# Grouping the value products of an attention and mixture-of-experts kernel by three key chunks instead of two

## The chip, the cores and the metric

One core of one Trainium2 chip runs the whole program. The metric is the device time of one execution in microseconds (us). The engines are named as in the profile: PE is the matmul engine (PEld its weight loads), DVE the vector engine, ACT the scalar engine, POOL the GpSimd engine, and SP issues DMAs.

## What is computed

Two batches, eight heads, 768 positions, head size 64, all in float32. Scores are masked by a six-bit hash of queries and keys:

```python
q_bits = (einsum('bhsd,dk->bhsk', q, proj) > 0)      # the same for k
mask = q_bucket[:, :, :, None] == k_bucket[:, :, None, :]
scores = where(mask, scale * q @ k.T, -1e9)
attn = exp(scores - max(scores)); attn = attn / (sum(attn) + 1e-9)
x = (attn @ v)                                        # to [1536, 512]
h = ((x @ w1) * (x @ w2)) @ w3;  y = h @ w_out        # dense layer
e = argmax(y @ w_gate + modality_bias[modality_id])   # one of 8 experts
out = gate * (relu(y @ W1[e]) @ W2[e])
```

The change lies in the attention part alone, which shares its time with the preparation of the dense layer (the product of w3 and w_out, called W34 here).

## The kernel before, in words

**Units and slots.** The function `body` handles pairs of heads: eight pairs, p = 0 to 7. A pair has twelve units of stage 1 and twelve units of stage 2. The main loop (`for i in range(NU + LEAD + NLAG + 1)`, NU = 96) runs over slots i. In slot i it issues, on each engine's queue in the order of the code, pieces of many things that are in different stages of progress. What follows is one slot, in that order.

- **Stage 1** of unit i (`stage_1`, L346 and L354, while i < 96): two matmuls give the scores of 128 queries against all keys, and DVE takes the row maximum (L354). After the last of every six units POOL makes the correction for the maxima of a half of the queries (L358 to L361, tile `fin`).
- **A step of the weight preparation on DVE** (`fill`): each of 40 raw weight pieces takes three DVE steps (L516, L517, L506), then for 24 of them an ACT copy and a POOL subtraction (L493, L494, `split`), which make the operands of W34. In a "long" slot, `fill` runs a second time here, and more `fill` calls stand behind stage 2 for slots outside the grouped region or when the list of steps is longer than two.
- **W34 matmuls** (`w34_step`, L599): up to nine 128x512 matmuls, by an allowance that grows by 3.35 each slot, and none in a long slot. After 24 matmuls a block is done. Then ACT copies it out (L602, `ev`), the next slot transposes it (`w34_t`, L574, `wt`), a later long slot does the gate matmuls (`w34_gate`, L582, `pg`), and the slot after that transposes those (`w34_sum`, L590, `pt`).
- **The transposes of the maxima** (`stage_f`, L366): three PE transposes bring the maxima of a half into the rows of the query operand, and two ACT copies (L369) write them there. They are issued in the slot `fi = i - 1` with `fi % 6 == 0`, so two slots after the last maximum of the half.
- **Value products** (`stage_a`, L392): the product of one key chunk's exponentials with the values, for both heads of the pair side by side in 64 columns each; four PE records of 385 columns. In slots with j = i - 9 from 18 to 97 they are issued only where `j % RUN == 1`, so two units together in every second slot.
- **Sums** (`stage_n`, L407): eight matmuls for the sums of a pair, in the slot NLAG units after its last unit of stage 2, then an ACT copy, DMAs and, for each batch, reciprocals on DVE (L419 to L424, the function `recip` from the list `late`).
- **Hashes** (`hash_half`, L259 and L272): for two coming pairs together, eight matmuls and one DVE operation per half of the positions, in the slots with i % 12 of 4 and 6 (`HASH`) of every second pair. The bits go to the operands by DMA (`d_bits`, from SP) in slots with i % 12 of 6 and 8.
- **Stage 2** of unit j (`stage_2`, L378, L379, L384): four matmuls give the transposed scores of one key chunk, ACT takes the exponential (L379) into one of four buffers `pt`, and POOL adds it to a running sum (L384).

**What couples the engines.** The two score tiles in PSUM (tag `s`) alternate between stage 1 and stage 2. So stage 1 of slot i + 1 waits for the maximum of slot i, and stage 2 of a slot waits for the exponential of the slot before. The tiles of `stage_f`, `w34_t`, `w34_gate`, `w34_sum`, `stage_n` and `hash_half` all have one PSUM buffer with the tag `m`, so each of them waits until ACT or DVE has read the one before.

**Long slots.** `grouped(i)` holds for slots 27 to 88, and `is_long(i)` for those of them that issue value products together. Before the change these are the even slots 28 to 88. `free_tail` puts the gate matmuls into a long slot that has no sums and (before) is not 1 modulo 6. The lower half of the queries (`q_lo`, L299 on DVE) is put at the head of the DVE list in slots with i % 12 = 6 and runs with the first `fill` of the next slot. In slots 78 to 89 `norm_0` (L656, L659, L661 on DVE) normalises the first quarter of the attention result. From slot 98 on, `moe_half` issues matmuls of the dense layer between the slots' other work.

The names that the change touches are these; everything else keeps its order.

Of the kernel before, what the change touches and what calls it, by code (L numbers as in the profile page):

```python
# [43 lines left out]
LEAD = 9  # L44
SOON = 17
AGE = 2
NLAG = 4
RUN = 2
NP = 4
BUSY = {4: (2, "m"), 5: (2, "m"), 6: (2, "a"), 7: (2, "a"), 8: (1, "a"), 9: (1, "a")}  # L50
GROUP = (18, 80)
AEND = 98
HASH = (4, 6)
PREL = 2
PREA = 2
SPLITS = (83, 84, 97, 98)
# [113 lines left out]
def body(tc, qT, kT, vP, w1d, w2d, w3d, wod, mod, wgate, mbias, e1, e2, cst, out):  # L170
# [65 lines left out]
    def load_pair(p):  # L236
        b, hp = divmod(p, HP)
        for nm, src in (("q", qT), ("k", kT)):
            t = r_raw([P, S])
            SP.dma_start(t, src[b, hp])  # L240
            raw_t[p, nm] = t
# [8 lines left out]
    def hash_half(pairs, half):  # L250
        hash_z(pairs, half)
        hash_bits(pairs, half)
# [88 lines left out]
    def stage_1(u):  # L341
        p, qt, hd = u
        q, k = head_t[p, hd, "q"], head_t[p, hd, "k"]
        s = ps("s", [P, 2, 512], f"m{p}_{qt}_{hd}")
        for half in range(2):
            PE.matmul(  # L346
                s[:, half, 0:HS], q[0:KROWS[hd], 0, qt * P:qt * P + P], k[0:KROWS[hd], 0, half * HS:half * HS + HS],
                start=True, stop=True,
            )
        if qt % 3 == 0 and hd == 0:  # L350
            nm_t[p, qt // 3] = r_nm([P, 32])
        nm = nm_t[p, qt // 3]
        at = 3 * (1 - hd) + qt % 3
        DVE.tensor_reduce(nm[:, at:at + 1], s[:, :, 0:HS], AX.XY, ALU.max, negate=True)  # L354
        if qt % 3 == 2 and hd == 1:
            v, fin = nm[:, 6:12], fins[qt // 3].bitcast(F32R).rearrange("p t (d c) -> p d t c", d=2)
            v3 = v.rearrange("p (d t) -> p d t", d=2)
            POOL.tensor_scalar(v, nm[:, 0:6], C_MASK / 2, None, ALU.is_lt)  # L358
            POOL.tensor_mul(v, v, nm[:, 0:6])
            POOL.tensor_copy(fin[:, :, :, 0], v3)  # L360
            POOL.tensor_sub(fin[:, :, :, 1], v3, fin[:, :, :, 0].bitcast(F32))  # L361
# [159 lines left out]
    def fill():  # L521
        if dq and isinstance(dq[0], int):
            dq[0:1] = piece(dq[0])
        if dq:
            dq.pop(0)()
# [13 lines left out]
    def grouped(i):  # L539
        return GROUP[0] <= i - LEAD < GROUP[1]  # L540

    def is_long(i):
        return grouped(i) and (i - LEAD) % RUN == 1

    def hashes(i):
        p, ph = divmod(i, 12)
        return p % 2 == 1 and p + 1 < NPAIR and ph in HASH

    def sums(i):
        n = i - LEAD - NLAG  # L550
        return 0 <= n < NU and n % 12 == 11

    def free_tail(i):
        while grouped(i) and (not is_long(i) or i % 6 == 1 or sums(i)):
            i += 1
        return i

# [13 lines left out]
    def w34_t(f, ev):  # L571
        t = ps("m", [P, 4, P], f"wt{f}")
        for c in range(4):
            PE.transpose(t[:, c, :], ev[:, c * P:c * P + P], ident)  # L574
        wT = r_wT([P, 4, P])
        ACT.copy(wT, t)
        tail_at.setdefault(free_tail(slot[0] + 1), []).append(lambda: w34_gate(f, wT))
# [35 lines left out]
    def w34_step(n, share=1):  # L613
        if 2 * slot[0] + share < w34_at[0]:
            return
        while n and done["w"] < len(w34q) and order.index(9 + 2 * w34q[done["w"]][0]) < done["n"]:
            w34q[done["w"]][1]()
            done["w"] += 1
            owed[0] -= 1
            n -= 1  # L620
            if done["w"] % 24 == 0:
                w34_at[0] = 2 * slot[0] + share + 2
                break
# [163 lines left out]
    sunits = [(p, half, c) for p in range(NPAIR) for half in range(2) for c in range(QT)]  # L787
    for i in range(NU + LEAD + NLAG + 1):
        slot[0] = i
# [54 lines left out]
        long = is_long(i)  # L844
        if i < NU:
            if p and ph == 9 and p + 3 < NPAIR:
                load_pair(p + 3)
            stage_1(units[i])
            fill()
            if long:  # L850
                fill()
        if p == 0 and ph in (1, 2):
            hash_z([1], ph - 1, "uw"[ph - 1])
# [7 lines left out]
        elif not long:  # L861
            quota = done["w"] + min(W34_MOST, int(owed[0]))
            w34_step(quota - done["w"], 0)
        fi = i if i <= 6 else i - 1
        if fi % 6 == 0 and 0 < fi <= NU and (i <= 6 or fi > 6):
            stage_f(*divmod(fi // 6 - 1, 2))
        for fn in todo_at.pop(i, []):
# [1 line left out]
        if hashes(i):  # L869
            for fn in tail_at.pop(i, []):  # L870
                fn()
        alone = not GROUP[0] <= j < AEND or j % RUN == 1
        while alone and next_a[0] <= min(j - AGE, NU - 1):
            stage_a(next_a[0])
            next_a[0] += 1
        for fn in tail_at.pop(i, []):
            fn()
        n = j - NLAG
        if i == NU + LEAD + 2:
# [3 lines left out]
        if hashes(i):  # L883
            hash_half([p + 1, p + 2], HASH.index(ph))
        if 0 <= j < NU and i != SOON:
# [664 lines left out]
```

## Time and profile before

| | |
|---|---|
| median of three executions | 673.7 us (673.34 to 673.91) |
| the profiled execution | 673.39 us, of which its span is 671.3 us |
| PE busy | 644.8 us, 96% of the span |
| DVE busy | 383.0 us, 57% |
| ACT busy | 319.4 us, 48% |
| POOL busy | 320.8 us, 48% |
| PE clock granted | full in all 40 slices of the page |
| slots 13 to 26 | 31.4 to 67.4 us after the span's start |
| slots 27 to 77 | 67.4 to 221.2 us |
| slots 78 to 90 | 221.2 to 261.0 us |

The span runs from the first instruction to the last; some 2 us of the device time lie around it. The slots are found in the trace by the first matmul of stage 1 (L346). Matmuls are pipelined, and each lasts longer in the trace than the distance to the next one, so that work on PE is read from start to start. A busy share says how long an engine had something to do, and not whether anybody waited for it.

### The profile page before, as it was taken

What the parts mean: (1) busy time and instruction counts of PE and PEld (TensorE: products, weight loads), DVE (VectorE), ACT (ScalarE), POOL (GpSimd) and SP (SyncE); (2) the same over time, 40 slices, a digit from 0 to 9 for tenths busy, and PEclk for the clock granted to TensorE, in tenths of its full rate; (3) what the DMA queues carried; (4) which work ended last, traced back from release to release, by engine and by line L of the source; (5) the groups of instructions that cost most, each with busy time, mean ns of one, the idle gap of its engine ahead of it and who ended that gap; (6) DMA issues with size and microseconds to landing.
All of it is one profiled execution on the core that took longest, in us unless ns stands there. A gap on an engine that the chain in (4) does not pass through costs nothing. (4 is left out here: it accounts for less than half of the span.)

```text
span 671.3 us, 10130 instructions
## 1 busy us (share of the span) xinstructions
PE 644.8 (96%) x3650; PEld 507.9 (76%) x3650; DVE 383.0 (57%) x573; ACT 319.4 (48%) x510; POOL 320.8 (48%) x291
## 2 busy tenths in 40 slices
PE   7998999999999999999999999999999999999995
PEld 2544666666666665687988988998888899899984
DVE  6798777667786999833521311211385865575550
ACT  7367575666556655753421211211124655565551
POOL 7598988686869777766241340420125012201110
PEclk9999999999999999999999999999999999999999
DMA  7747472664647484313301001000047886766630
GB/s 229 234 148 176 152 247 92 179 187 135 209 127 212 130 239 138 113 48 104 98 17 56 24 0 48 1 1 31 5 166 237 295 276 236 232 213 209 216 115 19
DMA packets 40663, 93.88 MB, mean 140 GB/s; under 512 B 6544, under 2 KB 11008, under 8 KB 40608
## 3 DMA queue, kind: packets, MB, share of 16 engines
q1 hardware_dynamic: 38528, 86.62, 41.7%
q0 software_dynamic: 2080, 6.56, 2.8%
q8 instruction: 31, 0.51, 0.3%
q14 instruction: 24, 0.20, 0.1%
HBM read 72.98 MB, written 12.94 MB: 128 GB/s over the span
## 5 line engine op out<-in xcount | busy, mean ns | idle before, releaser
L684 PE MATMUL ab<-x,w 128*128 128x384 f32 x512 | 135.3, 339 | 0.6 <-ACT ss L411 0.6
L384 POOL TENSOR_TENSOR acc<-acc,pt 128x770 f32<-128x770 f32 x64 | 119.9, 1874 | 21.5 <-ACT pt L379 19.9
L354 DVE TENSOR_REDUCE nm<-m 128x1 f32<-128x768 f32 x96 | 91.4, 955 | 49.7 <-PE m L346 49.2
L379 ACT ACTIVATE pt<-s 128x768 f32<-128x768 f32 x96 | 78.0, 812 | 71.9 <-PE s L378 69.7
L684 PEld LDWEIGHTS ab<-x,w 128*128 128x128 f32 x512 | 93.4, 188 | 5.8 <-issue 4.4
L378 PE MATMUL s<-q,k 128*128 128x384 f32 (+1 forms) x384 | 91.0, 359 | 4.0 <-ACT pt L379 3.8
L378 PEld LDWEIGHTS s<-q,k 128*128 128x128 f32 (+1 forms) x384 | 63.6, 189 | 38.7 <-issue 16.2
L696 POOL TENSOR_TENSOR g<-gf,g 128x384 fp32r<-128x384 f32 x32 | 32.9, 1029 | 125.1 <-ACT g L695 121.5
L684 PE MATMUL ab<-xlo,w 128*128 128x384 f32 x256 | 86.4, 338 | 0.0
L1214 DVE TENSOR_TENSOR eu<-er,eu 128x1024 fp32r<-128x1024 f32 x56 | 67.4, 1223 | 22.3 <-ACT eu L1213 20.8
L392 PE MATMUL a<-pt,v 128*64 128x385 f32 x384 | 74.5, 502 | 0.0
L1405 POOL DMA_INDIRECT out<-o,sidx x13 | 13.6, 1046 | 123.2 <-ACT o L1404 106.8
L1379 PE MATMUL e1F<-ex,eu 128*128 128x256 f32 x576 | 69.8, 282 | 0.5 <-DVE ex L1343 0.3
L1379 PEld LDWEIGHTS e1F<-ex,eu 128*128 128x128 f32 x576 | 69.2, 189 | 1.4 <-DVE ex L1343 0.5
L1397 PE MATMUL e2F<-eu,h 128*128 128x512 f32 x288 | 68.8, 394 | 0.0
L694 DVE TENSOR_TENSOR gf<-asb,ab 128x384 f32<-128x384 f32 x32 | 17.7, 554 | 84.0 <-PE ab L684 83.3
L1397 PEld LDWEIGHTS e2F<-eu,h 128*128 128x128 f32 x288 | 53.2, 188 | 11.2
L1213 ACT CAST eu<-er 128x1024 fp32r<-128x1024 f32 x56 | 57.6, 1047 | 5.9 <-DMA er<-e 5.4
L1023 PE MATMUL x2p<-w,g 128*128 128x512 f32 x240 | 57.4, 396 | 0.0
L346 PE MATMUL m<-k,q 78*128 78x384 f32 x192 | 52.4, 355 | 4.4 <-DVE nm L354 2.8
L1023 PEld LDWEIGHTS x2p<-w,g 128*128 128x128 f32 x240 | 44.8, 188 | 10.8 <-issue 0.6
L599 PE MATMUL w<-wo,w 128*128 128x512 f32 x192 | 49.0, 393 | 0.4 <-POOL w L494 0.4
(207 smaller groups left out, 869.5 us busy)
## 6 DMA issues: line engine op xcount, KB each, us to landing
er<-e SPq DMA_DIRECT2D x56, 512.0 KB
cr<-w3d SPq DMA_DIRECT2D x16, 512.0 KB
cr<-wod SPq DMA_DIRECT2D x8, 512.0 KB
cr<-w1d SPq DMA_DIRECT2D x8, 512.0 KB
wfd<-cT SPq DMA_DIRECT2D x16, 256.0 KB
cr<-w2d SPq DMA_DIRECT2D x8, 512.0 KB
st<-wfd SPq DMA_DIRECT2D x16, 256.0 KB
raw<-kT SPq DMA_DIRECT2D x8, 384.0 KB
```

The costliest lines, as they stand in the source:

```text
L346: PE.matmul(s[:, half, 0:HS], q[0:KROWS[hd], 0, qt * P:qt * P + P], k[0:KROWS[hd], 0, half * HS:half * HS + HS], start=True, stop=True,)
L354: DVE.tensor_reduce(nm[:, at:at + 1], s[:, :, 0:HS], AX.XY, ALU.max, negate=True)
L378: PE.matmul(s[:, hd, 0:HS], k[0:n, i, c * P:c * P + P], q[0:n, i, cl], start=(i == 0), stop=(i == 1))
L379: ACT.activation(pts[j % NP][:, :, 0:HS], s[:, :, 0:HS], AF.Exp, scale=SCALE)
L384: POOL.tensor_add(acc, pts[(j - 1) % NP] if c == 1 else acc, pts[j % NP])
L392: PE.matmul(a_t[p, half][64 * hd:64 * hd + 64, :], v[:, c, 64 * hd:64 * hd + 64], pts[j % NP][:, hd, :], start=(c == 0), stop=(c == QT - 1 ...
L684: PE.matmul(t, w12[j][:, st, c, fs], x[mv][:, c, :], start=(c == 0 and i == 0), stop=(c == 3 and i == 2))
L1023: PE.matmul(st["ps"], g_t[ch, f // 4][:, a, f % 4, i * P:i * P + P], w34[b][:, f, :], start=(f == 0 and k == 0), stop=(f == 7 and k == 2),)
L1213: ACT.copy(t[:, 0, sl], raw)
L1214: DVE.tensor_sub(t[:, 1, sl], raw, t[:, 0, sl].bitcast(F32))
L1379: PE.matmul(o[f], w[:, st, c, fs], x[:, mv, c, :], start=(c == 0 and i == 0), stop=(c == 3 and i == 2))
L1397: PE.matmul(o, h[:, st, f, sl], w[:, mv, f, :], start=(f == 0 and k == 0), stop=(f == 7 and k == 2))
```

## The change

Seven places, all in `body` and its constants:

```diff
-NLAG = 4
-RUN = 2
+NLAG = 5
+RUN = 3
...
-HASH = (4, 6)
+HASH = (4, 7)
...
     def free_tail(i):
-        while grouped(i) and (not is_long(i) or i % 6 == 1 or sums(i)):
+        while grouped(i) and (not is_long(i) or sums(i)):
             i += 1
         return i
...
             stage_1(units[i])
             fill()
-            if long:
+            for _ in range(RUN - 1 if long else 0):
                 fill()
...
-        fi = i if i <= 6 else i - 1
+        fi = i if i <= 6 else i - 2
         if fi % 6 == 0 and 0 < fi <= NU and (i <= 6 or fi > 6):
             stage_f(*divmod(fi // 6 - 1, 2))
```

Value products are issued for three units in every third slot (28, 31, ... 106). These slots are the long ones up to 88, so that W34 matmuls have two slots of three. A long slot has three DVE steps behind its maximum. The transposes of the maxima move one slot later, to the slots 14, 20, 26 and so on, which are never long. The sums of a pair and what hangs on them (the reciprocals in slot 65, now 66) move one slot later, the second half of the hashes from i % 12 of 6 to 7. Gate matmuls may stand in any long slot without sums. The loop has one more slot at its end.

## Rows read from the trace of the kernel before

**Rows 1.** Busy time by stretch: stretch and length, PE, PEld, DVE, ACT, POOL, then clock:

```profile
31.40:67.40 36.00, 32.10 (x165) 16.78 (x166) 31.61 (x41) 24.24 (x37) 31.92 (x28) 1.00 0.62 167
67.40:221.20 153.80, 149.09 (x840) 101.97 (x839) 110.72 (x144) 93.71 (x142) 122.41 (x100) 1.00 0.57 171
221.20:261.00 39.80, 36.45 (x203) 23.21 (x201) 38.29 (x47) 21.17 (x33) 28.46 (x27) 1.00 0.60 179
```

**Rows 2.** Timeline of PE, slots 26, 27, 28: start, length, line, operation, count, idle before:

```profile
65.40 0.51 PE L346 MATMUL m<-k,q 78*128 78x384 f32 x2
...
67.44 0.51 PE L346 MATMUL m<-k,q 128*128 128x384 f32 x2
68.56 0.97 PE L378 MATMUL s<-q,k 78*128 78x384 f32 x4 [0.61 <-ACT pt L379]
69.37 0.52 PE L346 MATMUL m<-k,q 78*128 78x384 f32 x2
...
72.07 0.52 PE L346 MATMUL m<-k,q 128*128 128x384 f32 x2
```

**Rows 3.** Timeline of PE, slot 33, a short slot with six W34 matmuls:

```profile
84.64 0.51 PE L346 MATMUL m<-k,q 128*128 128x384 f32 x2
84.99 1.53 PE L599 MATMUL w<-wo,w 128*128 128x512 f32 x6
86.36 0.86 PE L378 MATMUL s<-q,k 78*128 78x384 f32 x4
87.06 0.34 PE L346 MATMUL m<-k,q 78*128 78x384 f32 x1
```

**Rows 4.** Timeline of PE, slot 55, transposes of maxima and of gates together:

```profile
152.10 0.34 PE L366 MATMUL f<-ident,fin 128*66 128x128 f32 x3
153.50 0.33 PE L590 MATMUL pt<-ident,wT 128*128 128x128 f32 x1 [1.05 <-ACT q L369]
153.59 0.95 PE L378 MATMUL s<-q,k 78*128 78x384 f32 x4
```

**Rows 5.** Timeline of PE, slot 44, transposes of a W34 block:

```profile
117.57 0.66 PE L574 MATMUL wt<-ident,ev 128*128 128x128 f32 x4 [0.38 <-ACT q L369]
118.15 1.51 PE L392 MATMUL a<-pt,v 128*64 128x385 f32 x8
```

**Rows 6.** Waits of PE from 31.4 to 261 us: in total, times, longest:

```profile
PE s L378 <- ACT pt L379: 3.0, 6, 0.6
PE m L346 <- DVE nm L354: 2.8, 6, 0.8
PE f L366 <- POOL fin L361: 1.7, 2, 0.9
PE wt L574 <- ACT q L369: 1.4, 3, 0.6
...
PE wt L574 <- ACT ev L602: 0.7, 1, 0.7
```

**Rows 7.** Timeline of POOL, the second half of W34's first w3 block:

```profile
77.01 1.29 POOL L494 TENSOR_TENSOR w<-cT,w 128x512 fp32r<-128x512 f32 x1
```

**Rows 8.** Timeline of DVE, slots 66 and 67:

```profile
183.25 1.00 DVE L419 TENSOR_SCALAR sr<-sr 128x48 f32<-128x48 f32 x1
...
185.72 0.95 DVE L354 TENSOR_REDUCE nm<-m 128x1 f32<-128x768 f32 x1
...
187.30 0.70 DVE L516 TENSOR_SCALAR u<-cr 128x512 int32<-128x512 int32 x1
187.90 0.67 DVE L272 TENSOR_SCALAR bt<-z,cs 128x384 fp32r<-128x384 f32 x1
...
189.38 2.46 DVE L299 TENSOR_TENSOR lo<-raw,lo 128x768 fp32r<-128x768 f32 x1
```

**Rows 9.** Groups of PE from 67.4 to 221.2 us: count, busy, mean ns:

```profile
L259 PE MATMUL z<-raw,cs 128*32 128x384 f32 x32 | 3.4, 498 | 0.0
L582 PE MATMUL pg<-wT,wgs 128*32 128x128 f32 x48 | 2.6, 285 | 0.0
```

## The prediction

> **What bounds the kernel now.** I read the busy times by stretch first, then PE's waits, then the timeline slot by slot. Between slots 27 and 77 PE is busy for 149.09 of 153.80 us at full clock; DVE (110.72) and POOL (122.41) have room on average. In slots 78 to 90 DVE is busy for 38.29 of 39.80 us, and in slots 13 to 26 DVE (31.61 of 36.00) and POOL (31.92) are as full as PE (32.10) [rows 1]. So PE time counts in the middle, and DVE's list counts on both sides of it.
>
> Inside the middle the slots are regular. Stage 1 takes 84.99 - 84.64 = 0.35 us, a W34 matmul (86.36 - 84.99) / 6 = 0.228, stage 2 87.06 - 86.36 = 0.70 [rows 3]; stages 1 and 2 together are 1.05. Slot 26 with one value product lasts 67.44 - 65.40 = 2.04, slot 28 with two 72.07 - 69.37 = 2.70 [rows 2]. A product is thus 0.66 us, and going into the 64-column matmuls and out again costs 2.04 - 1.05 - 0.66 = **0.33 us per group**, however large. Slot 27 holds nothing but stages 1 and 2, yet lasts 69.37 - 67.44 = **1.93 us**: stage 2 waits for the exponential of the slot before [rows 2]. That is the floor of a slot; PE work of less than 1.93 gains nothing. A long slot is far above it (2.70), a short one only if W34 or something else fills 0.88 us.
>
> **The change, part by part.**
>
> *Fewer groups.* From slot 28 on, the products come in 40 groups before (28, 30, ... 106) and 27 after (28, 31, ... 106). 13 x 0.33 = **-4.3 us**. The number of products is the same.
>
> *More short slots that are not full.* The W34 matmuls are 192 in both cases, in 30 short slots before and 40 after (29 to 87). How many each slot gets follows from the loop's own book-keeping: 3.35 more each slot, at most 14 saved up, at most 9 at once, a stop at each 24 and until the pieces are made. The same count for the kernel before gives the six of slot 33 [rows 3]. After the change, a first short slot mostly gets 7 to 9, the second often 3. I list the slots whose PE work is under 1.93 us, with what they lose (an f transposition counted as 0.28, between the 0.34 that it lasts in [rows 4] and less, since it is pipelined; the transpose of gates 0.14; a wt 0.44, less than its 0.66 in [rows 5], as its end overlaps).
> Before: 27, 35, 87, 93, 95 empty (0.88 each); 89 with a transpose of gates (0.74); 37 and 91 with f (0.60); 97 with f and no stage 1 (0.95); 51 with one step (0.65); 65 with two (0.43). Sum 8.4.
> After: 27, 36, 87, 90, 93, 95 empty (5.3); 96 empty and without stage 1 (1.23); 35 and 89 (1.5); 86 and 92 with f (1.2); 50 with f and a step (0.37); 33, 42, 57 with wt (1.3); 63 with two steps (0.43); 48, 54, 66, 69, 71, 75 with three (0.20 each, 1.2). Sum 12.5.
> Difference **+4.1 us**: the floor takes back almost all that the groups give.
>
> *Transposes of the maxima and gates in one slot.* Maxima's transposes go to slots 6m + 2, right behind the long slots 6m + 1. Without the exclusion in `free_tail`, gate matmuls may land in 6m + 1, and their transpose then falls in 6m + 2. There it needs the same PSUM buffer, which ACT must first read twice: slot 55 is the one such slot before, with 1.05 us of idle PE, about 1.22 with what the drain costs [rows 4]. After, it is slots 44, 68 and 80: two more, **+2.4**.
>
> *Transposes of a W34 block behind f.* Before, three of them waited 1.4 us in all (slots 44, 80, 86) [rows 6], some 2.1 in slot time, as 0.38 of idle goes with 0.6 of a longer slot. After, f and wt meet so in slots 33 and 57, where ACT's copies delay the exponential too: 0.5 each beyond the floor. **-1.1**. The wait for ev (0.7, slot 66 above all) [rows 6] goes as the block now ends elsewhere, with 0.2 or so left in slots 43 and 64: **-0.6**.
>
> *A wait for POOL, in slot 30.* In the first W34 block the 13th matmul needs the second half of the first w3 piece. POOL, late by some slots, makes it until 78.30 [rows 7]. Before, that matmul is in slot 31, after 78.95, and waits for nothing. After, slot 30 (from 75.91, its start before) is short and has matmuls 10 to 17; the 13th would start at 75.91 + 0.35 + 3 x 0.228 = 76.95. POOL has the same list up to there, so PE waits 1.35: **+1.4** (0 if POOL is earlier by as much, 2 if the PE queue behind delays ACT too).
>
> *Three DVE steps in a long slot, with q_lo and a hash.* Slots 31, 43, 55, 67 and 79 are long now and have the maximum (0.96), q_lo (2.46), two steps (0.70 each) and in 43 and 67 the hash's comparison (0.67) [rows 8]: 4.8 to 5.5 us against 3.4 to 4.6 of PE. Mostly this is made good in the next slot, since PE has W34 matmuls there. Not so in slot 67: the reciprocals (185.72 - 183.25 = 2.47) [rows 8] now start in slot 66, a short one of 1.93. DVE leaves slot 66 about 2.7 into slot 67 and ends the comparison at 2.7 + 0.9 + 2.4 + 1.4 + 0.6 = 8.0. PE's slot 67 is 1.05 + 0.33 + 3 x 0.66 + 0.85 (hash, 3.4 / 4) + 0.43 (gates, 2.6 / 6) [rows 9] = 4.6; in slot 68 it reaches f, which wants that PSUM buffer, at 4.6 + 0.35 + 7 x 0.228 = 6.5. It waits 1.5: **+1.5** (0 to 2.5).
>
> *Slots 78 to 90.* DVE is full in both kernels. Following its list from slot 78, with stage 1 waiting for the maximum, I get waits of 0.3, 0.2, 1.2, 0.8 and 0.3 in slots 81, 83, 84, 87 and 90, against some 2.1 us before, of which [rows 6] show a part as waits for the maximum: **+0.7** (-1.5 to +2).
>
> *Slots 13 to 26.* f waited 1.7 us there for POOL's fin [rows 6], and one slot later it would not. But DVE is full, and slots wait for it as it is: I take -0.2 in slot 25 and nothing in slot 19. In slot 14 f now stands right ahead of the stage 2 that first needs it: two ACT copies less the value product between, +0.3. **+0.1** (-1.7 to +1).
>
> *At no cost.* The sums, their copy and DMAs a slot later, with five slots to the reciprocals as before; SP's `d_bits` behind the later comparison, and the loads behind it on SP, have four slots until stage 1 reads them. If that cover went, stage 1 of the next pair would wait by the DVE delay, up to 1.5 us three times. The added last slot is empty.
>
> Sum: -4.3 + 4.1 + 2.4 - 1.1 - 0.6 + 1.4 + 1.5 + 0.7 + 0.1 = **+4.2 us**. Of the last three plus terms I trust the size less, and take +3.6 in all. The sum is made against the profiled execution (673.39; span 671.3 and 2.1 around it), 0.3 under the median. **677.0 us.**
>
> **Rivals.**
>
> 1. *PE is the bound throughout.* If stage 2 can start without the wait of slot 27 (because the exponential comes earlier in a pair of short slots), and the new waits cancel the old, the groups' 4.3 us come out: 669.1. The wait of slot 27 speaks against it [rows 2], the steady 0.33 for it. The Trainium skill, TensorEngine Tiling (Array Packing), Key Properties, has it that a change of tiling mode drains the array while a change of tile does not; by that rule alone the saving would be by groups, and the trace agrees as to the price of a group. Chance 0.15.
>
> 2. *It comes out even.* Floor and groups cancel (-0.2), and the waits that go (1.7 us on fin, 2.8 for the maximum, 2.1 behind ACT [rows 6]) make up for those that come: 673 to 675. The sizes in slots 30 and 68 decide; with both at nothing the sum is +1.3. Chance 0.22.
>
> 3. *DVE becomes the bound.* If the three steps of a long slot and q_lo delay each maximum so that stage 1 waits in the following slot at 31, 43, 55 and 67, by about 1 us each, beyond my sum: 681. Against it: DVE's 110.72 of 153.80 [rows 1]. Chance 0.08.
>
> PE's clock is at its upper level (1.00, 2.4 GHz) in all three stretches, through idle times of up to 1.05 us [rows 1, 4]. I expect none of the new waits, up to 1.5, to change that, and take the chance as 0.02, within rival 3's. The Trainium skill, TensorE: Matmul & The Clock Gate (Part 1), says that the clock goes to half when the engine has been idle; that would speak against the change, but these waits did not bring it about.
>
> That the change does not do what it says I exclude: exponentials of four units fit the four buffers, as the first of three products is read in the slot that overwrites it, ahead of it on PE.
>
> **How the numbers follow.** The forecast, slower by +1.4 to +6 us, has the rest, 0.55. A measurement of this kernel can tell some 0.2%, 1.35 us. Faster: rival 1 and the lower edge of rival 2, 0.18. Same: most of rival 2, 0.20. Slower: 0.62. The range goes from 671.5 (a part of rival 1, with the gain half taken back) to 680.0 (the upper bounds of slots 30 and 68).
>
> **What would show it.** PE busy in the middle should fall by 3 to 4 us, and its waits for the exponential rise from six [rows 6] to some twenty. Slots 36, 48, 54, 66, 69, 71 and 75 should each last 1.93. PE's waits of pt for ACT should be three, of about 1.05; one wait of W34 for POOL of 1.35 in slot 30; f in slot 68 should wait for DVE's comparison. Waits of f for fin should be gone. I am wrong if those slots fall below 1.9, or if stage 1 waits for the maximum in most slots behind a long one.

## The result, and the profile after

The changed kernel takes **679.6 us** (median of six executions, 677.87 to 681.05); the kernel before, beside it, 673.41 (six, 673.22 to 673.91). The ratio is 1.0091, with a 95% interval from 1.0079 to 1.0102: slower by 6.2 us. The forecast was slower, 677.0, with a range to 680.0. The profiled execution took 679.62 us, its span 677.5 against 671.3.

Where the 6.2 us come is seen from the first matmul of stage 1 of a slot in both traces. Slot 27 starts 0.15 us later than before, slot 40 5.06 later, slot 66 6.00, slot 78 6.64, slot 91 only 4.13, and from 313 us on everything is 6.13 later. So most of it is lost in slots 27 to 39, 1.6 more in slots 40 to 77, 2.5 are won back in slots 78 to 90, and 2.0 are lost again at the end of the attention (1.3 of the two are work that moved: two value products).

Busy times of the kernel after in the stretches that answer to [rows 1], slots 13 to 26, 27 to 77 and 78 to 90, in the same columns:

```profile
31.37:67.59 36.22, 31.60 (x165) 16.99 (x166) 30.81 (x41) 24.00 (x37) 32.07 (x27) 1.00 0.58 159
67.59:227.83 160.24, 151.59 (x842) 103.76 (x841) 110.51 (x146) 94.54 (x145) 121.93 (x101) 0.99 0.55 170
227.83:265.08 37.25, 33.73 (x192) 22.44 (x191) 34.51 (x45) 20.54 (x32) 28.31 (x27) 1.00 0.62 190
...
195.58:200.53 4.95, 3.33 (x18) 2.56 (x18) 4.17 (x7) 2.38 (x4) 3.07 (x2) 1.00 0.46 122
200.53:204.20 3.67, 3.67 (x14) 2.93 (x15) 1.55 (x2) 2.08 (x3) 1.83 (x1) 0.56 0.28 77
```

The middle has grown from 153.80 to 160.24 us. DVE and POOL are busy for what they were there, and PE is idle for 8.65 us of it instead of 4.71. The last two lines are slot 68 and what follows it. After slot 68, in which PE was idle for 1.62 us, the granted clock is 0.56 for 3.67 us (for the most part the lower level, 1.2 GHz). Before, it was full in the whole attention.

PE's waits of the kernel after, from 31.4 to 266 us, answer to [rows 6]:

```profile
PE s L378 <- ACT pt L379: 4.1, 10, 0.6
PE pt L590 <- ACT q L369: 3.2, 3, 1.1
PE m L346 <- DVE nm L354: 1.9, 5, 0.7
PE w L599 <- POOL w L494: 1.9, 3, 0.8
PE f L366 <- DVE bt L272: 1.8, 2, 1.3
PE m L346 <- ACT pt L379: 1.6, 2, 1.0
PE s L378 <- ACT q L369: 1.2, 1, 1.2
PE wt L574 <- ACT q L369: 0.7, 2, 0.4
```

The wait for `fin` (1.7) and that for `ev` (0.7) are gone, and wt behind f is halved. W34 waits for POOL's pieces in three slots, before only in slot 29 (0.42). The gates' transposes wait behind f three times (1.05 each) instead of once. New are f's waits for DVE's hash comparison in slots 20 (1.27) and 68 (0.57), and that of stage 2 in slot 14 for ACT's copies of f (1.2).

PE's timeline of the kernel after, cut to slots 20, 27, 29 to 31, 39 and 68 to 70, answers to [rows 2 to 4]:

```profile
50.93 0.34 PE L366 MATMUL f<-ident,fin 128*66 128x128 f32 x3 [1.27 <-DVE bt L272]
...
67.59 0.51 PE L346 MATMUL m<-k,q 128*128 128x384 f32 x2
68.72 0.97 PE L378 MATMUL s<-q,k 78*128 78x384 f32 x4 [0.61 <-ACT pt L379]
69.52 0.52 PE L346 MATMUL m<-k,q 78*128 78x384 f32 x2
...
74.03 1.88 PE L599 MATMUL w<-wo,w 128*128 128x512 f32 x7 [0.81 <-POOL w L494]
...
76.81 1.32 PE L599 MATMUL w<-wo,w 128*128 128x512 f32 x5
78.89 0.97 PE L599 MATMUL w<-wo,w 128*128 128x512 f32 x3 [0.76 <-POOL w L494]
...
80.40 0.51 PE L346 MATMUL m<-k,q 128*128 128x384 f32 x2
80.84 2.16 PE L392 MATMUL a<-pt,v 128*64 128x385 f32 x12
82.93 0.97 PE L378 MATMUL s<-q,k 78*128 78x384 f32 x4
83.75 0.52 PE L346 MATMUL m<-k,q 78*128 78x384 f32 x2
...
105.32 0.62 PE L346 MATMUL m<-k,q 128*128 128x384 f32 x2 [1.01 <-ACT pt L379]
107.42 0.97 PE L599 MATMUL w<-wo,w 128*128 128x512 f32 x3 [0.31 <-POOL w L494]
...
198.27 0.34 PE L366 MATMUL f<-ident,fin 128*66 128x128 f32 x3 [0.57 <-DVE bt L272]
199.67 0.33 PE L590 MATMUL pt<-ident,wT 128*128 128x128 f32 x1 [1.05 <-ACT q L369]
...
202.06 1.49 PE L378 MATMUL s<-q,k 78*128 78x384 f32 x4
203.34 0.84 PE L346 MATMUL m<-k,q 78*128 78x384 f32 x2
```

Slot 27 lasts 1.93 us again, and so do slots 35, 36, 42, 48, 54, 66, 71, 89 and 92. Slot 31, with three products, lasts 83.75 - 80.40 = 3.35, and 1.05 + 0.33 + 3 x 0.66 = 3.36: a product and a group cost what they did. Four matmuls of stage 2 take 203.34 - 202.06 = 1.28 us at the lower clock, against 0.70.

**The account.** I take each slot's length less the larger of 1.93 us and its PE work at the prediction's prices (it has none for the sums of a pair, which are taken at the 0.8 us by which they lengthen a slot). What is left is what waits and clock cost. Summed over slots 27 to 94 that floor is 196.6 us after and 196.4 before, so groups and floors cancel as forecast. What is left over is 12.3 us after and 6.6 before. The difference by parts, with the forecast beside it:

| | forecast | measured |
|---|---|---|
| groups and floors | -0.2 | +0.2 |
| gates' transposes behind f (44, 68, 80; before 55) | +2.4 | +2.3 |
| wt behind f, and the wait for ev | -1.7 | -2.2 |
| W34 waits for POOL in slot 30 | +1.4 | +1.1 |
| f in slot 68 waits for the hash comparison | +1.5 | +0.7 |
| slots 78 to 90, apart from the above | +0.7 | -0.5 |
| slots 13 to 26 | +0.1 | +0.15 |
| slot 29 (W34 waits 0.81 for POOL, before 0.42) | 0 | +0.4 |
| slots 38 and 39 | 0 | +1.9 |
| clock in slots 69 and 70 | 0 | +1.3 |
| slots 91 to 94 (slot 93 waits 0.99 for the exponential) | 0 | +0.6 |

The sum is 5.95; some 0.2 more are in small pieces.

### The profile page after: what moved, and what is told of

Its sections match the earlier page's. It is cut to its first block, busy times and chain, and to the rows that moved or that the text cites. A ratio compares the mean times of both kernels' runs of the same rounds, so it can differ in the third digit from the quotient of the medians.

```text
span 677.5 us, 10131 instructions
## 1 busy us (share of the span) xinstructions
PE 644.4 (95%) x3650; PEld 509.9 (75%) x3650; DVE 380.9 (56%) x573; ACT 319.0 (47%) x510; POOL 320.1 (47%) x291
## 3 DMA queue, kind: packets, MB, share of 16 engines
q0 software_dynamic: 2080, 6.56, 2.8%
## 5 line engine op out<-in xcount | busy, mean ns | idle before, releaser
L392 PE MATMUL a<-pt,v 128*64 128x385 f32 x384 | 71.7, 499 | 0.0
L599 PE MATMUL w<-wo,w 128*128 128x512 f32 x192 | 51.4, 400 | 1.9 <-POOL w L494 1.9
```

What stands on the lines that cost most here:

```text
L392: PE.matmul(a_t[p, half][64 * hd:64 * hd + 64, :], v[:, c, 64 * hd:64 * hd + 64], pts[j % NP][:, hd, :], start=(c == 0), stop=(c == QT - 1 ...
```

## The experiments

Where a line number is one higher than in the listing, the edit put a line ahead of it. Times are medians; the kernel before ran beside each.

**1. Gate matmuls kept out of slots 6m + 1** (a_excl). The changed kernel with the old condition:

```diff
-        while grouped(i) and (not is_long(i) or sums(i)):
+        while grouped(i) and (not is_long(i) or i % 6 == 1 or sums(i)):
```

> The changed kernel with the exclusion of slots 6m + 1 for gate matmuls put back. Theory (waits for the one PSUM buffer): the three transposes of gates behind the transposes of maxima (slots 44, 68, 80) go elsewhere, 1.05 us of idle and 1.2 of slot time each, and with slot 68's idle gone the half-rate clock of slots 69 and 70 (1.3 us) does not come: 3.6 to 5 us less than the changed kernel, about 675 us. Rival (the cost of the change is in short slots that wait for the exponential, and in POOL): within 1 us of the changed kernel, 679.

674.61 us, ratio 1.0020 (1.0010 to 1.0029): 5.0 under the changed kernel. PE's timeline of it in slots 44 and 68:

```profile
124.04 0.35 PE L366 MATMUL f<-ident,fin 128*66 128x128 f32 x3
124.23 0.92 PE L378 MATMUL s<-q,k 78*128 78x384 f32 x4
...
196.88 0.35 PE L366 MATMUL f<-ident,fin 128*66 128x128 f32 x3 [0.60 <-POOL acc L384]
197.06 0.93 PE L378 MATMUL s<-q,k 78*128 78x384 f32 x4
```

No transpose of gates stands between f and stage 2 any more. Slots 44, 68 and 80 go from 4.69, 4.95 and 4.25 us to 3.36, 3.81 and 2.92: 3.8 us in all, gate matmuls and transposes that moved elsewhere among it. Slot 68 still waits 0.60 for f (the row names POOL, but DVE's hash comparison ends 0.14 us ahead of f, as in the changed kernel). The clock stays up behind it, and slots 69 and 70 go from 6.60 to 5.66. Without the meetings of the two transposes, the fall of the clock included, the changed kernel is thus only 1.2 us over the kernel before, which itself has one such meeting, in slot 55. What slots 27 to 39 lose is untouched: slot 40 starts 41.30 us after slot 27, before the change 36.43.

**2. The gates' transpose behind stage 2** (a_pt). The same two transposes in the same slots, the second one issued later:

```diff
-        after(1, lambda: w34_sum(f, wT))
+        sum_at.setdefault(slot[0] + 1, []).append(lambda: w34_sum(f, wT))
...
             stage_2(j)
+            for fn in sum_at.pop(i, []):
+                fn()
```

> The changed kernel, gates where it puts them, but with the transpose of the gates issued behind stage 2 of its slot instead of ahead of it. Theory (in slots 44, 68 and 80 PE only waits for ACT to read the one PSUM buffer): 0.7 us of stage 2 covers most of each 1.05, the half-rate clock behind slot 68 becomes rarer, 2 to 3.5 us less than the changed kernel, 676 to 677.5. Rival (it was the gates' place that cost, by what else they meet there): within 0.7 us of 679.6.

676.80 us, ratio 1.0045 (1.0029 to 1.0062): 2.8 under the changed kernel. PE's timeline of it, end of slot 68:

```profile
198.76 0.33 PE L590 MATMUL pt<-ident,wT 128*128 128x128 f32 x1 [0.28 <-ACT q L369]
198.85 0.59 PE L346 MATMUL m<-k,q 128*128 128x384 f32 x2
```

The three waits of 1.05 become 0.30, 0.28 and 0.30, and slots 44, 68 and 80 are 0.8 us shorter each. So the price was the place of the transpose, which held stage 2 on PE's queue until ACT had read f twice. Slots 69 and 70 take 5.16 us at full clock. In this profile the clock fell later instead, behind the wait of 0.99 us in slot 93, and slots 93 and 94 took 7.21 us against 6.05 in experiment 1, about half of the 2.2 us by which this kernel stays above it.

**3. Longer work in eight short slots** (a_dup). The score matmuls of stage 1 are issued three times over in slots 27, 35, 36, 87, 89, 90, 93 and 95. They give the same scores again, and PE has 0.70 us more in each:

```diff
+DUP = (27, 35, 36, 87, 89, 90, 93, 95)
...
-        for half in range(2):
+        for half in (0, 1) * (3 if slot[0] in DUP else 1):
```

> The changed kernel with the matmuls of stage 1 issued three times over (same operands, same place) in the eight short slots 27, 35, 36, 87, 89, 90, 93 and 95: 0.70 us more PE work in each. Theory (such a slot lasts 1.93 us whatever PE does in it, as stage 2 waits for the exponential): 0 to 0.7 us more than the changed kernel, the wait for the exponential down from 0.6 to nothing. Rival (PE's work is the bound in these slots too): 5.6 us more.

679.92 us, ratio 1.0095 (1.0076 to 1.0114), 0.3 over the changed kernel, which the two intervals can't tell apart. PE's timeline of it, slots 36 and 39:

```profile
94.64 1.31 PE L347 MATMUL m<-k,q 78*128 78x384 f32 x6 [0.19 <-DVE nm L355]
...
97.01 0.45 PE L347 MATMUL m<-k,q 128*128 128x384 f32 x1 [0.35 <-DVE nm L355]
...
107.01 0.96 PE L600 MATMUL w<-wo,w 128*128 128x512 f32 x3 [0.72 <-POOL w L495]
```

PE is not the bound in those slots: 0.70 us of work costs 0.33 in slot 27 (2.26) and 0.35 in slot 35. It is not free either, as I had reckoned up to 0.88, since the added copies put the maximum off, and now stage 1 waits for that. And what the added work cost in slots 27 to 37 (1.3 us) came back before slot 40, which starts 41.34 us after slot 27 in this kernel and 41.35 in the changed one. W34 waits less in slot 29, and slots 38 and 39 take 7.28 us instead of 8.17, up to the same piece of POOL's.

**4. A PSUM buffer for each stage's scores** (a_sbuf). In slot 39 stage 1 waits 1.01 us for an exponential, because the buffers of tag `s` have changed places. With a tag of one buffer for each stage they can't:

```diff
-nbuf = {"s": 2, "m": 1}
+nbuf = {"s1": 1, "s2": 1, "m": 1}
...
-        s = ps("s", [P, 2, 512], f"m{p}_{qt}_{hd}")
+        s = ps("s1", [P, 2, 512], f"m{p}_{qt}_{hd}")
...
-        s = ps("s", [P, 2, 512], f"s{p}_{half}_{c}")
+        s = ps("s2", [P, 2, 512], f"s{p}_{half}_{c}")
```

> The changed kernel with a PSUM tag of its own for the score tiles of stage 1 and for those of stage 2, so that neither can take the other's buffer. Theory (in slot 39 stage 1 got the buffer that the exponential of slot 38 still read): the wait of 1.01 us goes, slot 38 lasts 3.4 instead of 4.55, and the wait in slot 18 goes too; 1.2 to 1.8 us less than the changed kernel. Rival (POOL is late there and the wait moves behind it): slots 38 to 40 together as long as before, 0 us.

688.00 us, ratio 1.0220 (1.0202 to 1.0239). Much of the 8.4 us over the changed kernel has another cause: slots 0 to 5, where stage 1 had both buffers to itself, are 4.8 longer, and the clock fell near 16 and 50 us. The wait in slot 18 did not go either: slots 17 and 18 take 6.56 us instead of 3.97. Only slots 38 to 40 are to be compared. PE's timeline of slot 39 in this kernel:

```profile
111.39 1.33 PE L599 MATMUL w<-wo,w 128*128 128x512 f32 x5
114.28 0.96 PE L599 MATMUL w<-wo,w 128*128 128x512 f32 x3 [1.57 <-POOL w L494]
```

Stage 1 no longer waits, and W34 waits 1.57 us for POOL instead of 0.31. Slots 38 to 40 take 12.27 us against 12.30, and slot 40 starts 41.32 us after slot 27. So the theory is out and the rival holds: the changed places of the buffers cost nothing there, and POOL's piece sets when slot 39 ends.

**5. Two w3 blocks off POOL** (a_split). DVE makes the subtractions of the first two w3 blocks, four pieces:

```diff
+ONDVE = (8, 9, 11, 13)
...
-            POOL.tensor_sub(lo, T, hi.bitcast(F32))
+            (DVE if k in ONDVE else POOL).tensor_sub(lo, T, hi.bitcast(F32))
```

> The changed kernel with the subtractions of the first two w3 blocks (four of 24) on DVE instead of POOL. Theory (W34 matmuls of the first blocks reach their operands before POOL has them): the waits of W34 for POOL in slots 29, 30 and 39 (0.81, 0.76, 0.31 idle; 2.2 us and more in slot time) go and nothing takes their place, 2 to 3 us less than the changed kernel. Rival (DVE is as late there): the waits move to DVE, within 0.7 us of the changed kernel.

681.13 us (four executions, 680.02 to 686.15), ratio 1.0140 (1.0097 to 1.0183), whose interval meets that of the changed kernel. PE's timeline of slot 30:

```profile
78.25 0.62 PE L347 MATMUL m<-k,q 78*128 78x384 f32 x2 [1.81 <-DVE nm L355]
78.71 2.02 PE L600 MATMUL w<-wo,w 128*128 128x512 f32 x8
```

W34 waits for nothing in slots 29 and 30, and slots 38 and 39 take 6.36 us instead of 8.17. But the maxima come later: stage 1 waits 1.81 for one in slot 30, and 0.96 in slots 27, 36 and 37 (there for the exponential). Slot 40 starts 0.67 us later than in the changed kernel. So no time is won by giving DVE these pieces of POOL's work.

**6. Products also in slots without W34** (b_dyn and a_exdyn). If a slot has no W34 matmul it would be empty; here it gets the products that are due. Once on the kernel before, once on the changed kernel with the edit of experiment 1:

```diff
+        w_then = done["w"]
...
         alone = not GROUP[0] <= j < AEND or j % RUN == 1
+        alone = alone or (i < EARLY and (i >= SWITCH - 1 or done["w"] == w_then))
```

> The kernel before with value products issued also in slots (before 98) in which no W34 matmul was ready: 27, 35, 37, 87, 89, 91, 93, 95, 97, one product each, so that the groups are more and smaller. Theory (a short slot without W34 matmuls lasts 1.93 us anyway, so a product of 0.66 and its group's 0.33 cost 0.1 to 0.4 there and save 0.66 in the next long slot): 2.5 to 4.5 us less than the kernel before, 669 to 671. Rival (each group costs 0.33 wherever it stands): 9 x 0.33 = 3 us more, 676.

> The changed kernel with the exclusion put back (674.6 by itself) and value products also in slots before 98 without a W34 matmul (27, 33, 35, 36, 42, 57, 86, 87, 89, 90, 92, 93, 95, 96). Theory (short slots wait for the exponential): 3.5 to 6 us less than with the exclusion alone, 668.5 to 671. Rival (each group costs 0.33 wherever it stands): 3 us or more above 674.6.

On the kernel before 673.38 us, ratio 1.0003 (0.9994 to 1.0013). On the other 672.86, ratio 0.9996 (0.9986 to 1.0005), 1.7 under experiment 1. PE's timeline of the first, slots 27 to 30:

```profile
67.29 0.51 PE L346 MATMUL m<-k,q 128*128 128x384 f32 x2
...
73.37 1.88 PE L599 MATMUL w<-wo,w 128*128 128x512 f32 x7 [1.00 <-POOL w L494]
...
75.78 0.51 PE L346 MATMUL m<-k,q 78*128 78x384 f32 x2
```

Both theories missed in time, and so did the rivals. The slots behave as expected: 27 and 28 take 4.10 us instead of 4.63. The time doesn't. Slot 29 waits 1.00 for POOL instead of 0.42, and slot 30 starts 8.49 us after slot 27, against 8.47 before. In the other kernel slot 40 starts 41.72 us after slot 27 (41.30 in experiment 1), with W34 waits of 1.38, 0.71 and 1.20. What is left of its gain comes later. In these places PE time saved ahead of a piece of POOL's was only waited for.

**7. A slower pace of W34** (a_pace, a_pace0, b_pace). At most six matmuls in a slot, so that fewer are asked for before their piece exists, and the second short slot has some left:

```diff
-W34_MOST = 9
+W34_MOST = 6
```

With the edit of experiment 1:

> The changed kernel with the exclusion put back and at most six W34 matmuls in a slot instead of nine. Theory (with two short slots of three, W34 runs ahead of the operands that POOL makes, and leaves the second short slot empty): the waits of W34 for POOL in slots 30 and 39 go (0.8 and 0.3 idle, about 2 us with slots 38 to 40), and fewer slots have three or less: 1 to 3 us less than with the exclusion alone, 671.5 to 673.5. Rival (POOL and DVE bound slots 27 to 40 whatever the order of W34): within 0.7 us of 674.6.

671.21 us, ratio 0.9974 (0.9958 to 0.9990), 3.4 under experiment 1. PE's timeline of it, slot 30:

```profile
75.79 0.51 PE L346 MATMUL m<-k,q 78*128 78x384 f32 x2
76.14 1.55 PE L599 MATMUL w<-wo,w 128*128 128x512 f32 x6
```

Slot 30 takes 2.43 us instead of 3.96, without a wait. Slot 40 starts 3.9 us earlier than in experiment 1 (1.1 of it are five W34 matmuls put off), and slot 78 4.0, with 167 W34 matmuls done against 168: the gain lies in slots 29 to 39, and later short slots have room for what was put off. In this profile the clock fell behind slot 93, so that 2.4 us are left of it by slot 95; the medians have 3.4. Without that edit:

> The changed kernel with at most six W34 matmuls in a slot and the exclusion left out as the change has it. Theory (the two effects are independent): the 3.4 us that pacing gave with the exclusion, 676.2, with the three waits of 1.05 us for ACT if the gates still land in slots 6m + 1, or less if the other pace moves them away. Rival (pacing only helps once the waits are gone): within 1 us of 679.6.

673.51 us (ten executions, 671.57 to 676.47), ratio 1.0001 (0.9989 to 1.0012). I had expected 3.4 under the changed kernel; it is 6.1. The blocks end in other slots, and only slot 68 still has both transposes, so that two meetings of some 1.2 us go as well. The profiled execution is the slowest of the ten: the clock fell in it behind slot 68 again, and also in slots 20 and 36. On the kernel before, as a control:

> The kernel before with one edit: at most six W34 matmuls in a slot instead of nine. A control for the after-kernel with the gate exclusion put back and the same pace of six (671.21 median). Theory: the gain of 3.4 us that the pace gave there belongs to the grouping by three, whose first short slots were given seven to nine matmuls that POOL's pieces were late for, and left a second short slot nearly empty. In the kernel before each short slot already gets six or seven (slot 33 six), so the limit moves little: 673.4, between 672.5 and 674.5, and its slot 33 still has six. Rival: a slower pace is worth the same under either grouping, because it lets POOL's pieces come in time everywhere: then 670 to 671, and the grouping by three has no part in beating the kernel before.

674.03 us, ratio 1.0013 (1.0004 to 1.0022). The time is as the theory had it, the reason isn't. By slot 78 this kernel is 10.1 us ahead of the kernel before, with 144 W34 matmuls done instead of 165 (the 21 put off are 4.8 us), and loses all of it in slots 78 to 94. PE's waits of it in slots 78 to 90:

```profile
PE m L346 <- DVE nm L354: 4.3, 6, 1.2
PE m L346 <- ACT pt L379: 1.4, 1, 1.4
```

With every second slot a short one, 192 matmuls in 30 slots need 6.4 a slot, and six are too few. The control thus only says that this pace, as it stands, gains nothing under groups of two. A pace of seven there was not tried, so whether groups of three are needed for the gain at all stays open.

**8. The maxima's transposes alone** (b_f and a_pace13). The kernel before with that one shift, and the kernel of a_pace with the first late one of them back in slot 13:

```diff
-        fi = i if i <= 6 else i - 1
+        fi = i if i <= 6 else i - 2
...
-        fi = i if i <= 6 else i - 2
+        fi = i if i <= 6 else i - (1 if i < 18 else 2)
```

> The kernel before with nothing changed but the transposes of the maxima one slot later (two units behind the last maximum). Theory (this part is nearly free; its cost in the change came from gates that met it): slot 55 loses its 1.2 us, slot 14 gains a wait of 1.2 for ACT, the waits for POOL's fin in slots 19 and 25 go, but DVE is full there: 672 to 674. Rival (the shift itself costs, by slot 14 and by what ACT does later): 675 or more.

> The changed kernel with the exclusion and the pace of six, and the first late transposes of maxima (slot 14) back in slot 13, the others two units behind as changed. Theory (slot 14's wait of 1.21 for ACT is a loss of its own): 0.8 to 1.3 us less than 671.2. Rival (DVE is full from slot 16 to 25 and stage 1 waits for it instead): slot 27 begins within 0.3 us of the same time, 671.2.

The shift by itself: 673.19 us, ratio 1.0000 (0.9990 to 1.0010). Slot 14 waits 1.21 us behind ACT's copies, the waits for `fin` go, and slot 55 falls from 4.73 to 3.28, as f no longer stands there. Other slots that now have f are longer (38 by 0.86, 56 by 0.69), and the sum is nothing, as the theory had it. PE's timeline of it, slots 55 and 56:

```profile
154.17 0.27 PE L590 MATMUL pt<-ident,wT 128*128 128x128 f32 x1
154.20 0.95 PE L378 MATMUL s<-q,k 78*128 78x384 f32 x4
...
155.84 0.35 PE L366 MATMUL f<-ident,fin 128*66 128x128 f32 x3 [0.34 <-DVE wgp L591]
```

The second: 671.35 us (ten executions, 669.50 to 673.32), ratio **0.9972 (0.9961 to 0.9983)**. Slot 14 takes 2.26 instead of 3.66 and slot 27 starts 1.25 us earlier. The median is no better than that of a_pace, so the expected 0.8 to 1.3 us do not show in it. Its profiled execution, without a fall of the clock in the attention, took 669.74; its ten mean granted clocks run from 0.992 to 0.998, and the two fastest executions (669.50 and 669.74) have the two highest. These two kernels beat the one before by 0.3% and the changed one by 1.2%.

## Why the prediction was right, and where it was not

**Direction and range.** Slower was right, and 679.6 lies inside the range, near its end. The size was not: 3.3 us over the median were forecast, and 6.2 came. That the time still lies in the range is in part luck. The range's end was reckoned from slots 30 and 68, which cost less than forecast (1.8 us for 2.9); what took the time there are parts that I had put at nothing, 4.2 us in all. Rival 2, that it comes out even, is out: slots 30 and 68, which were to decide, were smaller than I had them, and the ratio's interval still begins at 1.0079.

**Groups and floors: right.** Of the short slots that I had listed as under-filled, those that no other term touches last 1.93 to 2.00 us; 86, 87, 90 and 93 are longer (2.1 to 2.6). Products of three cost 0.33 once; this is the first check of that price, since the prediction solved for a product and a group from two slots. Floors and groups cancel, so the change had next to nothing to gain in this form: rival 1 is out. Experiment 3 shows that the floor is not PE's work; that it is the chain of score, exponential and maximum is read from the waits. One slot is shorter, slot 91 of the kernel before with 1.67, whose own start waits 0.28 for a maximum. Experiment 3 corrects one thing: the 0.88 us of free room under it holds for work that stands behind stage 1's scores, and not for work that delays the maximum.

**Gates' transposes behind f: right.** Forecast +2.4, measured +2.3, in the three slots named, with the wait of [rows 4] again. Experiments 1 and 2 show the mechanism.

**wt and ev: right**, -2.2 for -1.7. Slots 33 and 57 are 0.48 beyond the floor, for 0.5.

**Slot 30: right, with a wrong step.** W34 waits 0.76 there for the piece of [rows 7]. I had three matmuls ahead of it; the trace has five. In the code the 13th and 14th matmul of the block read what ACT copies, and the 15th is the first to read what POOL subtracts. Slot 30 starts 0.54 later, POOL 0.55 later. Slot time +1.1 for +1.4.

**Slots 13 to 26: right in the sum** (+0.15 for +0.1), by larger pieces than I had: slot 14 waits 1.21 us behind ACT, where I had 0.3, f in slot 20 waits 1.27 us for the hash comparison, which I had looked for in slot 68 alone, and the waits for `fin` (1.7) go.

**Slot 68: too high.** The wait of f for the comparison is 0.57 and not 1.5. DVE leaves the reciprocals later than I had it (3.3 us into slot 67, not 2.7), but q_lo, priced at 2.46, lasts 0.95 there:

```profile
195.27 0.95 DVE L299 TENSOR_TENSOR lo<-raw,lo 128x768 fp32r<-128x768 f32 x1
```

In slots 31 and 43 of the same trace it lasts 2.55; what makes the difference was not tried.

**Slots 78 to 90: wrong sign**, -0.5 for +0.7. DVE had 34.51 us of work there and not 38.29 [rows 1]; the largest part is that four products of the normalisation (L661) take 4.2 us instead of 6.5. No run took this apart. The slots win 2.5 us in all, as two products (1.3) and three W34 matmuls (0.7) fewer fall in them; slots 91 to 94 then have the two products more.

**Slots 29, 38 and 39: the step that failed most**, +2.3 where I had put nothing. I priced POOL's lateness at the first piece alone. Slot 29 waits longer for the half before it. In slots 38 and 39 the loop hands out nine and eight matmuls in a row, and the last three need a piece that POOL ends at 107.4:

```profile
106.08 1.28 POOL L494 TENSOR_TENSOR w<-cT,w 128x512 fp32r<-128x512 f32 x1
```

Experiments 3, 4 and 6 changed PE's work or the buffers ahead of such pieces, and each time the wait for POOL took up the difference; experiment 7 asked for them later, and 3.9 us went there, 1.1 of them work put off. Rival 3, DVE as the bound, is not what came: experiment 5 makes that case, and it looks different (stage 1 waits for the maximum).

**The clock: wrong.** I gave it 0.02, because idle times up to 1.05 us had left it up. Slot 68 has two of them, 0.57 and 1.05 us, with two pieces of PE work between, and 1.3 us went at 1.2 GHz behind it. The Trainium skill, TensorE: Matmul & The Clock Gate (Part 1: The HAM clock gate), says that the clock goes to half when the engine has been idle; the trace agrees in so far as the fall came behind these waits. It does not show that a wait is enough: single waits of 1.21, 1.27 and 1.05 us, in slots 14, 20, 44 and 80 of the same trace, left the clock up, and of the fourteen profiles only those with both waits in slot 68 have a fall behind it, and not all of them.

**Slots 91 to 94: not looked at.** Slot 93 is the second of two empty slots and lasts 2.59 us instead of 1.93, with a wait of 0.99 for the exponential. I took each empty slot at the floor; why this one is longer was not tried.

**The signs that I named.** The three waits of 1.05 came, f in slot 68 behind the comparison too, and no wait for `fin` is left. Slots 36, 48, 54, 66, 71 and 75 last 1.93 to 1.97; slot 69 ran on the slow clock. The wait in slot 30 came with 0.76 for 1.35, and W34 waits in two slots more. Two did not: PE busy between slots 27 and 77 rose by 2.5 us instead of falling by 3 to 4, and the waits for the exponential rose to ten and not to some twenty. The slow clock adds 1.3 us to it, and one product and three W34 matmuls more fall in the stretch (1.3 us); why the smaller number of groups does not show in it is open.

## What to carry to other kernels

When work is gathered into fewer, longer steps, count what the emptied steps last without it: here a chain of score, exponential and maximum keeps them at 1.93 us, and it gave back what the groups saved. The slots that are freed are worth something only if other work can fill them, so its pace has to be set anew against the engine that feeds it (here six in place of nine gave 3.4 us, while the same six gave nothing under groups of two). Where two short operations share a buffer that another engine must empty, look which of them stands ahead of the next long one on the queue: issued behind it, the wait was 0.3 us instead of 1.05.

## What the runs showed of the hardware

The granted clock fell to the lower level (1.2 GHz) behind PE idle times of a size that had left it up in the profile of before. Five profiles have both waits in slot 68 (0.54 to 0.86 and 1.05 us): in four of them the clock fell behind it (after, a_dup, a_sbuf, a_pace0), in a_split it did not. Eight profiles have a wait of about 1 us in slot 93: behind it the clock fell in a_pt, a_split and a_pace, and not in after, a_excl, a_sbuf, a_pace0 and a_pace13. Slot 94 in the kernel after and in a_pace, with the same PE work, in the columns of [rows 1]:

```profile
273.05:276.50 3.45, 3.45 (x19) 1.88 (x19) 3.45 (x5) 2.30 (x4) 0.85 (x1) 1.00 0.46 141
...
264.64:269.09 4.45, 4.45 (x19) 2.19 (x19) 3.61 (x5) 2.31 (x4) 0.65 (x1) 0.73 0.39 124
```

In a_pace0 the clock also fell in slot 20, behind a wait of 1.24 us, and in slot 36, behind two of 0.61; the kernel after has waits of 1.27, 0.49 and 0.62 there without a fall. So such a fall comes in some executions and not in others. Those of the kernel after spread over 3.2 us, the kernel before's over 0.7, and the shortest one (677.87) has the highest mean clock, 0.999, the longest (681.05) the lowest, 0.992. What decides whether it comes is not shown.
